# Pair 0's triangular inverses by products on TensorE, in place of column steps on VectorE through DRAM

## The chip, the cores and the metric

One core of a Trainium2 chip runs the whole kernel. The metric is device time in microseconds (us), lower is better. Six runs of the kernel before took 695.22 to 700.58 us, median 697.76. The engines are TensorE (PE: matmuls, with the weight loads PEld beside them), VectorE (DVE), ScalarE (ACT), GpSimd (POOL) and SyncE (SP), which here only issues DMAs. Each engine works through its own queue in order.

## The reference

A delta rule over 768 tokens (4 batches, 8 heads, head size 48), then a gated feed-forward layer:

```python
for t in range(S):
    kt, vt, bt = (k_n[:, :, t], v[:, :, t], beta[:, :, t, None])
    y[:, :, t] = np.einsum('bhd,bhde->bhe', q[:, :, t], state)
    v_old = np.einsum('bhde,bhd->bhe', state, kt)
    state = state + bt[:, :, :, None] * np.einsum('bhd,bhe->bhde', kt, vt - v_old)
...
h = x @ w_in
g = h * np.cos(h)
return (g @ w_out).astype(np.float32)
```

`k_n` is the key divided by its norm; `x` is y with the heads side by side (3072 x 384), `w_in` is 384 x 2048, `w_out` 2048 x 384. Both weight matrices come as 64-bit floats.

## The kernel before

The 768 steps are cut into 24 units of 32 tokens (C = 32), two units to a pair. Within a unit, all steps are solved at once: with G the products of the unit's keys, scaled by beta and cut to its strictly upper triangle, the unit needs the inverse of I + G, a 32x32 triangular matrix for each of 32 (batch, head) blocks. The blocks of a unit lie as 128 partitions (4 batches x 32) by 8 heads x 32.

For a unit `n` of pair `m` the work runs so: load k, q (L337), square, sum and root for the norms (ACT L456, DVE L461, POOL L473, then five small DVE operations L484 to L492); transpose k and q (PE L514) and copy them (`kq_t`, ACT L524); `gram` (PE L545); `gram_keys` gives g (DVE L556), `gram_queries` gives tt (DVE L565). Then the inverse, per pair:

- `gram_put` (SP L576) writes g of both units to DRAM, `gram_get` (SP L585) reads it back with each block in one partition.
- `invert` goes through 31 columns, two operations for each (L614, L621). For pairs 1 to 11 it runs on POOL, with z in SBUF; for pair 0 it runs on DVE, with z in PSUM (`VECTOR = {0: "one"}`), and ACT copies z out (L625).
- `put` (SP L630) writes z to DRAM, `get` (SP L639) reads it back as `zt`, four DMAs for each unit.

Then `through_state` (PE L656), `right_side` (DVE L671), `solve` (PE L683: p_u from zt), `solve_out` (DVE L691), `update` (PE L704), `within` (PE L721), `features` (PE L738) with ACT copies between; a unit needs the state that the unit ahead of it left. When the features of a pair are there, its feed-forward starts: `hidden` in 8 steps (PE L759 for pair 0, in halves by unit; L776 for the others), the cosine on ACT and DVE, then the output (PE L823 for pair 0, and for the others seven products of half the size in Strassen's way, L881, with sums of weights in `w_sum`).

The weights are read in 28 tiles called `pairs` (SP L421; 12 for w_in, 16 for w_out), and each is turned into 32-bit floats by ACT (L429, L431), DVE (L435, L440) and POOL (`narrow_add`, L444). Hidden step k of pair 0 waits for the first 3(k+1) tiles.

The order on each engine isn't written by hand. Every piece of work is a task with an engine, an assumed cost and what it depends on (`add`); `Order.run` plays the tasks through, and each engine takes the ready task with the earliest due time. The tasks are emitted in that order, and each instruction is pinned behind the one ahead of it on its engine. If a task's data come later than was assumed, the engine waits at that place, and everything behind it waits too. The first loads are issued ahead of this: k of unit 0 and q of unit 1 on SP, q of unit 0 on ACT, the constants, beta and k of unit 1 on POOL.

Quoted with the line numbers of the profile:

## Time and profile before

| what | value |
|---|---|
| median of six runs | 697.76 us |
| the profiled execution | 700.58 us, span 698.8 us |
| busy PE | 628.8 us (90%) in 10,968 matmul records |
| busy weight loads | 556.5 us |
| busy DVE | 412.5 us (59%) |
| busy ACT | 264.6 us (38%) |
| busy POOL | 345.6 us (49%) |
| granted PE clock, mean | 0.99 |
| DMA | 52.41 MB, 213,009 packets |

The span counts from the first instruction to the last of the profiled execution; 1.8 us lie around it. A matmul in 32-bit floats shows as two records, so that `gram`, `solve` or `within` of a unit, 32 matmuls each, are 64 records. Busy time is an average over the whole run: what counts for an early change is how the first stretches look, and what ended each wait there.

### The profile page before, as it was taken

Reading aid. Unit: us, or ns where it says so; the run is one execution under the profiler, and the core shown is the slowest. Engines: PE = TensorE matmul, PEld = TensorE weight load, DVE = VectorE, ACT = ScalarE, POOL = GpSimd, SP = SyncE. Lnnn points to the kernel's source line nnn. Section 1 sums busy time; section 2 is a strip of 40 time slices with the busy share of each in tenths; the row PEclk is TensorE's granted clock in tenths of the full one; section 3 lists DMA queues with packets and bytes.
Section 4 is the critical chain, followed back from the end, with each engine's and each line's share of the span. In section 5 each row is a group of like instructions: output and inputs, shape, how many; then the busy total and the mean of one; then the engine's idle time right before and its main releaser. Section 6 shows DMA issues by size and latency. Waiting matters only on the chain.

```text
span 698.8 us, 25089 instructions
## 1 busy us (share of the span) xinstructions
PE 628.8 (90%) x10968; PEld 556.5 (80%) x10968; DVE 412.5 (59%) x820; ACT 264.6 (38%) x450; POOL 345.6 (49%) x738
## 2 busy tenths in 40 slices
PE   3306879998999999999999999999999999999997
PEld 2205768776888888888888898898888988988997
DVE  4885676975675555565565575565466454444542
ACT  4423746733252342342343343343432342433430
POOL 6469848851874824824824824823817608400000
PEclk9999979999999999999999999999999999999999
DMA  9886674455325324324334334235132130100000
GB/s 176 202 168 181 149 195 123 79 81 91 66 42 97 57 47 88 59 47 95 53 58 86 52 57 93 46 52 91 29 70 56 18 62 26 30 14 14 1 23 23
DMA packets 213009, 52.41 MB, mean 75 GB/s; under 512 B 204388, under 2 KB 207604, under 8 KB 212900
## 3 DMA queue, kind: packets, MB, share of 16 engines
q1 hardware_dynamic: 211428, 49.97, 36.5%
q8 instruction: 86, 1.41, 0.8%
q0 software_dynamic: 384, 0.64, 0.4%
q10 hardware_dynamic: 1088, 0.20, 0.1%
q14 instruction: 23, 0.19, 0.1%
HBM read 39.76 MB, written 11.01 MB: 73 GB/s over the span
## 4 chain that ended last, share of the span: by engine, by line
PE 77%; DVE 7%; DMA 6%; SPq 3%; issue 2%; POOL 2%; ACT 1%; ACTq 0%; DVEq 0%; POOLq 0%
PE p_h L776 29%; PE p_out L881 27%; PE p_kq L656 4%; PE p_h L759 4%; PE p_kq L721 3%; PE p_s L704 3%; PE p_u L683 3%; PE p_g L545 2%; SPq L348 2%; PE p_o L881 1%; DMA out_dram<-o 1%; SPq L337 1%; DMA kp<-in_k_dram 1%; DVE p_i L621 1%; PE p_out L823 1%
## 5 line engine op out<-in xcount | busy, mean ns | idle before, releaser
L776 PE MATMUL p_h<-x_ffn,w_in 128*128 128x256 f32 x1056 | 241.4, 381 | 1.3 <-DVE g_ffn L813 1.3
L614 POOL TENSOR_TENSOR part<-z,gb 128x126 f32<-128x126 f32 (+22 forms) x341 | 130.6, 383 | 207.3 <-DMA gb<-g_dr 171.6
L776 PEld LDWEIGHTS p_h<-x_ffn,w_in 128*128 128x128 f32 x1056 | 197.4, 190 | 28.1 <-PE p_t L514 1.1
L621 POOL TENSOR_TENSOR z<-z,part 128x126 f32<-128x126 f32 (+22 forms) x341 | 140.2, 411 | 26.7
L881 PE MATMUL p_out<-w_out,g_ffn 128*128 128x192 f32 x672 | 127.2, 335 | 0.8
L793 DVE SCALAR_TENSOR_TENSOR r<-p_h,turns 128x512 f32<-128x512 f32 x96 | 65.5, 687 | 99.2 <-ACT turns L789 99.2
L789 ACT ACTIVATE turns<-p_h 128x512 int32<-128x512 f32 x96 | 56.5, 592 | 165.9 <-PE p_h L776 148.0
L881 PEld LDWEIGHTS p_out<-w_out,g_ffn 128*128 128x128 f32 x672 | 109.6, 191 | 6.3 <-ACT o L918 3.0
L881 PE MATMUL p_out<-w_sum,g_ffn 128*128 128x192 f32 x496 | 89.0, 329 | 4.4 <-DVE o L931 4.4
L897 DVE TENSOR_TENSOR g_ffn<-g_ffn 128x256 f32<-128x256 f32 x176 | 78.5, 462 | 19.4 <-PE p_out L881 17.5
L800 ACT ACTIVATE r<-r 128x512 f32<-128x512 f32 x96 | 60.4, 629 | 76.6 <-DVE r L793 76.5
L881 PEld LDWEIGHTS p_out<-w_sum,g_ffn 128*128 128x128 f32 x496 | 81.6, 190 | 7.6 <-DVE o L931 6.1
L813 DVE TENSOR_TENSOR g_ffn<-r,p_h 128x512 f32<-128x512 f32 x96 | 65.1, 678 | 35.2 <-ACT r L801 35.0
L801 ACT ACTIVATE r<-r,halfpi 128x512 f32<-128x512 f32 x96 | 69.3, 722 | 3.1
L931 DVE SCALAR_TENSOR_TENSOR o<-p_out,o 128x192 f32<-128x192 f32 x74 | 25.3, 354 | 37.1 <-PE p_out L881 36.1
L514 PE MATMUL p_t<-consts,kp 128*128 128x128 f32 x32 | 7.3, 371 | 41.8 <-DVE tt L565 31.4
L514 PEld LDWEIGHTS p_t<-consts,kp 128*128 128x128 f32 x32 | 5.0, 188 | 43.2 <-issue 38.7
L473 POOL TENSOR_TENSOR knrm<-ksum,halves 128x16 f32<-128x16 f32 (+1 forms) x14 | 36.3, 2596 | 5.5 <-DVE ksum L461 3.2
L732 ACT COPY y<-p_kq 128x384 f32<-128x384 f32 x24 | 11.5, 478 | 65.0 <-PE p_kq L721 65.0
L656 PEld LDWEIGHTS p_kq<-st,kq_t 48*32 48x32 f32 x2944 | 29.7, 106 | 7.7 <-issue 7.0
L656 PE MATMUL p_kq<-st,kq_t 48*32 48x48 f32 x2944 | 33.3, 215 | 2.9 <-issue 2.8
L545 PEld LDWEIGHTS p_g<-kq_t 48*32 48x32 f32 x1536 | 18.2, 114 | 14.8 <-issue 12.7
(74 smaller groups left out, 611.5 us busy)
## 6 DMA issues: line engine op xcount, KB each, us to landing
pairs<-in_moe_w_in_dram SPq DMA_DIRECT2D x12, 512.0 KB
gb<-g_dr SPq DMA_DIRECT2D x24, 256.0 KB
pairs<-in_moe_w_out_dram SPq DMA_DIRECT2D x16, 384.0 KB
vp<-in_v_dram SPq DMA_DIRECT2D x96, 48.0 KB
kp<-in_k_dram SPq DMA_DIRECT2D x92, 48.0 KB
out_dram<-o SPq DMA_DIRECT2D x23, 192.0 KB
g_dr<-g SPq DMA_DIRECT2D x24, 128.0 KB
z_dr<-z SPq DMA_DIRECT2D x12, 256.0 KB
```

The lines of the kernel that those rows point to most:

```text
L473: nc.gpsimd.tensor_tensor(out=scales[m][2][:, part], in0=sums[m, part.start][:, 0:n], in1=halves[:, 0:n], op=ALU.pow,)
L614: eng.tensor_tensor(out=part, in0=z[:, 0:rows, j, None].to_broadcast(shape), in1=a[:, j, None, j + 1 :].to_broadcast(shape), op=ALU.mult,)
L621: eng.tensor_tensor(out=behind, in0=behind, in1=part, op=ALU.subtract)
L656: nc.tensor.matmul(p_kq[quarter(b), par, a, j], kq_t[rows48(par), a, b * NP + j], st[rows48(par), b // 2, j, b % 2], start=(j == 0 and a = ...
L776: nc.tensor.matmul(p_h[:, i], w_in[:, t, (f + i) * 128 : (f + i + 1) * 128], xts[p][:, t], start=(t == 0), stop=(t == KT - 1),)
L789: nc.scalar.activation(turns[p, f], p_hs[p, f], AF.Copy, scale=TURN)
L793: nc.vector.scalar_tensor_tensor(out=r, in0=p_hs[p, f], scalar=TURN, in1=turns.pop((p, f)), op0=ALU.mult, op1=ALU.subtract,)
L800: nc.scalar.activation(r, r, AF.Abs)
L801: nc.scalar.activation(r, r, AF.Sin, bias=halfpi, scale=-2.0 * math.pi)
L813: nc.vector.tensor_tensor(out=out, in0=rests.pop((p, f)), in1=p_hs.pop((p, f)), op=ALU.mult,)
L881: nc.tensor.matmul(p_o, left(p, e // 2, a)[:, e % 2], right(e, b), start=(e == 0), stop=(e == FT // 2 - 1), skip_group_check=True,)
L897: nc.vector.tensor_tensor(out=left(p, k, to), in0=left(p, k, one), in1=left(p, k, two), op=op)
```

## The change

For pair 0 alone, the two units' blocks are no longer sent through DRAM and inverted column by column. The 32x32 triangle is taken as two triangles of 16 (`parts[0]`, called D) and the square between them (`cross`, E). The triangles are inverted by doubling: X = I - D, then X = X + D^2 X, X + D^4 X, X + D^8 X, where the powers come from products 32x32 on PE (`power`, `grow`), each with copies by ACT and DVE and transposes of 32x32 blocks by DVE (`flip`). Two further products with the square (`border`) give the whole inverse, which is `zt`. All of it works in the memory of `w_sum` before the sums of weights are made there; the PSUM comes from tag "h". `invert_eye` and `invert` lose their DVE form; `gram_put`, `gram_get`, `put` and `get` remain for the pairs from 1 on.

The first loads are placed anew: k of units 0 and 1 on SP, q of both on ACT, and the large part of the constants behind beta on POOL. The planner's picture changes with it: the DMA queue is modelled by parts, matmuls cost 1.7 times as much until 4 us after the first hidden step, and start times and due times are others (`WINDOW`, `W_IN`, `W_OUT`, `LOADS`, `START`, `FIRST`, `STEP`), so that the order on every engine is a new one. In the changed order, as it is built, DVE has the flip of unit 0's first power behind the work on the third weight tile and the scales of unit 3; PE has all hidden steps of pair 0 ahead of the solve of unit 2, and all hidden steps of pair 1 and all output steps of pair 0 ahead of the solve of unit 4; SP has g of units 2 and 3 with one weight tile behind each, and the reads of z behind its write with one weight tile between (pair 1) or none (pair 2).

```diff
@@ -33,11 +33,15 @@
+    cross = (p[:, None] % C < C // 2) & (np.arange(C)[None, :] >= C // 2)
...
+            p[:, None] % C == np.arange(C)[None, :],
+            (p[:, None] % C < np.arange(C)) & ~cross,
+            cross,
@@ -54,18 +58,19 @@
-    WINDOW = 128.245
-    LAG = {"PE": 0.2, "DVE": 0.15, "ACT": 0.15, "POOL": 0.2, "SP": 2.0}
-    IN_FLIGHT = 8
+    WINDOW = 114.423
+    LAG = {"PE": 0.2, "DVE": 0.15, "ACT": 0.15, "POOL": 0.2, "SP": 2.0, "IN": 0.3}
+    IN_FLIGHT, ISSUE = 8, 0.49
+    SLOW, WARM = 1.7, 4.0
...
...
@@ -351,27 +359,27 @@
+    load(0, "q", nc.scalar)
+    load(1, "k")
+    load(1, "q", nc.scalar)
...
     consts_dr = nc.inline_tensor(consts_np, name="consts")
...
-    near = 130 + C
-    for cols in (slice(0, near), slice(near, consts_np.shape[1])):
-        nc.gpsimd.dma_start(out=consts[:, cols], in_=consts_dr.ap()[:, cols])
+    near = 130 + 4 * C
+    nc.gpsimd.dma_start(out=consts[:, 0:near], in_=consts_dr.ap()[:, 0:near])
...
-    eye = consts[:, 130 + C :].rearrange("p (r i) -> p r i", i=C)
-    load(0, "q", nc.scalar)
+    diag = consts[:, 130 + C : 130 + 2 * C]
+    parts = consts[:, 130 + 2 * C : near].rearrange("p (x i) -> p x i", i=C)
+    eye = consts[:, near:].rearrange("p (r i) -> p r i", i=C)
...
-    load(1, "q")
-    load(1, "k", nc.gpsimd)
+    nc.gpsimd.dma_start(out=consts[:, near:], in_=consts_dr.ap()[:, near:])
@@ -564,10 +572,101 @@
-            in0=p_gs.pop(n)[:, :, :, 1],
+            in0=p_gs[n][:, :, :, 1],
...
+    doubles = {}
+    def double(n, x):
+        if n not in doubles:
+            flat = w_sum.rearrange("p e x c -> p (e x c)")
+            at = n * 9 * H * C
+            doubles[n] = flat[:, at : at + 9 * H * C].rearrange(
+                "p (x h i) -> p x h i", x=9, i=C
+            )
+        at = "DWEFPQXRB".index(x)
+        return doubles[n][:, at] if len(x) == 1 else doubles[n][:, at : at + len(x)]
+    def mask_scale(n):
+        bs = scales[n // 2][0][:, n % 2]
+        nc.vector.tensor_tensor(
+            out=double(n, "RB"),
+            in0=bs[:, None, :, None].to_broadcast([128, 2, H, C]),
+            in1=parts[:, :, None, :].to_broadcast([128, 2, H, C]),
+            op=ALU.mult,
+        )
+    def mask_keys(n, x):
+        nc.vector.tensor_tensor(
+            out=by_parity(double(n, "DE"[x])),
+            in0=p_gs[n][:, :, :, 0],
+            in1=by_parity(double(n, "RB"[x])),
+            op=ALU.mult,
+        )
+        flip(double(n, "WF"[x]), double(n, "DE"[x]))
+    def flip(to, from_):
+        nc.vector.transpose(
+            to.rearrange("p h i -> p (h i)"), from_.rearrange("p h i -> p (h i)")
+        )
+    p_pows = {}
+    def products32(to, one, two):
+        for h in range(H):
+            for b in range(B):
+                nc.tensor.matmul(
+                    to[quarter(b), h], one[quarter(b), h], two[quarter(b), h]
+                )
+    def power(n, step):
+        if step == 0:
+            p_pows[n] = bank("h", [128, 2, H, C], "p_pow")
+        one, two = ("WD", "QP", "PW")[step]
+        products32(p_pows[n][:, 0], double(n, one), double(n, two))
+    def power_out(n, step):
+        if step < 2:
+            nc.scalar.copy(double(n, "P"), p_pows[n][:, 0])
+        else:
+            nc.scalar.copy(double(n, "Q"), p_pows[n][:, 0])
+    def power_flip(n, step):
+        flip(double(n, "QW"[step]), p_pows[n][:, 0])
+    def grow(n, step):
+        products32(p_pows[n][:, 1], double(n, "QWQ"[step]), double(n, "X"))
+    def less(to, one, two, op=ALU.subtract):
+        nc.vector.tensor_tensor(out=to, in0=one, in1=two, op=op)
+    def grow_out(n, step):
+        if step == 0:
+            wide = [128, H, C]
+            less(double(n, "X"), diag[:, None, :].to_broadcast(wide), double(n, "D"))
+        else:
+            less(double(n, "X"), double(n, "X"), p_pows[n][:, 1], ALU.add)
+        if step == 3:
+            flip(double(n, "R"), double(n, "X"))
+    def border(n, step):
+        to = p_pows[n][:, step]
+        if step == 0:
+            products32(to, double(n, "F"), double(n, "X"))
+        else:
+            products32(to, double(n, "R"), double(n, "B"))
+    def border_out(n, step):
+        if step == 0:
+            nc.scalar.copy(double(n, "B"), p_pows[n][:, 0])
+        else:
+            zts[n] = work.tile([128, H, C], FP, name="zt")
+            less(zts[n], double(n, "X"), p_pows.pop(n)[:, 1])
@@ -587,43 +686,31 @@
-    def invert_eye(m, tag):
-        if tag is None:
-            zs[m] = work.tile([128, ROWS, C], FP, name="z", bufs=ZS)
-        else:
-            zs[m] = bank(tag, [128, ROWS, C], "p_i")
+    def invert_eye(m):
+        zs[m] = work.tile([128, ROWS, C], FP, name="z", bufs=ZS)
         nc.scalar.copy(zs[m], eye)
-    def invert(m, tag, columns):
+    def invert(m, columns):
...
-        eng = nc.gpsimd if tag is None else nc.vector
...
-            if tag is None:
-                part = work.tile([128, ROWS * C // 2], FP, name="part")
-            else:
-                part = ffn_pool.tile([128, ROWS * C // 2], FP, name="part_v", tag="o")
+            part = work.tile([128, ROWS * C // 2], FP, name="part")
...
-            eng.tensor_tensor(
+            nc.gpsimd.tensor_tensor(
...
-            eng.tensor_tensor(out=behind, in0=behind, in1=part, op=ALU.subtract)
-    def invert_out(m):
-        z = work.tile([128, ROWS, C], FP, name="z", bufs=ZS)
-        nc.scalar.copy(z, zs[m])
-        zs[m] = z
+            nc.gpsimd.tensor_tensor(out=behind, in0=behind, in1=part, op=ALU.subtract)
     def put(m):
@@ -951,63 +1038,85 @@
-        free={"SP": 5.5, "ACT": 5.6, "POOL": 6.2, "DVE": 6.0, "PE": 6.0},
+        free={"SP": 4.5, "ACT": 6.2, "POOL": 5.6, "DVE": 4.0, "PE": 5.8},
...
-    VECTOR = {0: "one"}
-    W_IN, W_OUT, LOADS = 96.141, 47.302, -16.83
+    W_IN, W_OUT, LOADS = -9.302, 31.519, 0.897
...
+    COLD = 0.55
...
-    START = 68.004
-    FIRST, STEP = 4.724, 5.365
+    START = 42.564
+    FIRST, STEP = 3.024, 5.599
...
     def inverse(m):
...
-            each = (0.2, 0.001) if held else (0.323, 0.00178)
...
-                2 * (each[0] + each[1] * (j // SPLIT + 1) * (C - 1 - j)) for j in range(x, y)
+                2 * (0.323 + 0.00178 * (j // SPLIT + 1) * (C - 1 - j)) for j in range(x, y)
...
-            add(("inv", m, i), "DVE" if held else "POOL", cost,
-                lambda x=x, y=y: invert(m, held, range(x, y)), deps,
+            add(("inv", m, i), "POOL", cost, lambda x=x, y=y: invert(m, range(x, y)), deps,
...
-        if held:
-            add(("inv_out", m), "ACT", 0.65, lambda: invert_out(m), deps,
-                makes=[("z", ("z", m))], uses=[z])
-            deps = [("inv_out", m)]
...
+    def double_tasks(n, scaled):
+        add(("mask", n), "DVE", 0.7, lambda: mask_scale(n), [scaled])
+        add(("gram_keys", n), "DVE", 0.85, lambda: mask_keys(n, 0),
+            [("gram", n), ("mask", n)], uses=[("p_g", n), ("scales", n // 2)])
+        add(("grow_out", n, 0), "DVE", 0.45, lambda: grow_out(n, 0), [("gram_keys", n)])
+        add(("gram_cross", n), "DVE", 0.85, lambda: mask_keys(n, 1), [("gram_keys", n)],
+            uses=[("p_g", n)])
+        done = [("gram_keys", n)]
+        for i in range(3):
+            add(("power", n, i), "PE", COLD, lambda i=i: power(n, i), done,
+                makes=[] if i else [("h", ("p_pow", n))])
+            if i:
+                add(("grow", n, i), "PE", COLD, lambda i=i: grow(n, i - 1),
+                    [("power", n, i), ("grow_out", n, i - 1)])
+                add(("grow_out", n, i), "DVE", 0.46, lambda i=i: grow_out(n, i),
+                    [("grow", n, i)])
+            if i < 2:
+                add(("power_flip", n, i), "DVE", 0.46, lambda i=i: power_flip(n, i),
+                    [("power", n, i)])
+            add(("power_out", n, i), "ACT", 0.4, lambda i=i: power_out(n, i),
+                [("power", n, i)])
+            done = [("power_out", n, i)] + ([("power_flip", n, i)] if i < 2 else [])
+        add(("grow", n, 3), "PE", COLD, lambda: grow(n, 2), done + [("grow_out", n, 2)])
+        add(("grow_out", n, 3), "DVE", 0.85, lambda: grow_out(n, 3), [("grow", n, 3)])
+        add(("border", n, 0), "PE", COLD, lambda: border(n, 0),
+            [("grow_out", n, 3), ("gram_cross", n)])
+        add(("border_out", n, 0), "ACT", 0.4, lambda: border_out(n, 0), [("border", n, 0)])
+        add(("border", n, 1), "PE", COLD, lambda: border(n, 1), [("border_out", n, 0)])
+        add(("border_out", n, 1), "DVE", 0.46, lambda: border_out(n, 1),
+            [("border", n, 1)], makes=[("zt", ("zt", n))], uses=[("p_pow", n)])
     def unit(n):
...
-                add((x, n), "SP", 0.0, lambda: None)
...
-            deps = [(x, n - 1)] if n else []
-            if n == (0 if x == "v" else 4):
-                deps.append(("gram_get", 0))
+            deps = [(x, n - 1)] if n > (0 if x == "v" else 2) else []
+            if n == 4 and x != "v":
+                deps.append(("gram_get", 1))
...
-                (x, n), "SP", 1.9, lambda x=x: load(n, x), deps,
-                makes=[("vp", ("vp", m))] if x == "v" and not second else [], moves=1.6,
+                (x, n), "SP", 1.95, lambda x=x: load(n, x), deps,
+                makes=[("vp", ("vp", m))] if x == "v" and not second else [], moves=1.25,
@@ -1048,20 +1157,24 @@
-            makes=[(tag, ("p_g", n)), ("g_gram", ("g_gram", n)), ("tt", ("tt", n))],
+            makes=[(tag, ("p_g", n)), ("tt", ("tt", n))]
+            + ([("g_gram", ("g_gram", n))] if m else []),
...
-        add(("gram_keys", n), "DVE", 0.46, lambda: gram_keys(n),
-            [("gram", n), scaled],
-            uses=[("p_g", n), ("scales", m)])
+        if n < 2:
+            double_tasks(n, scaled)
+        else:
+            add(("gram_keys", n), "DVE", 0.46, lambda: gram_keys(n), [("gram", n), scaled],
+                uses=[("p_g", n), ("scales", m)])
...
-        add(("gram_put", n), "SP", 0.45, lambda: gram_put(n), [("gram_keys", n)],
-            makes=[] if second else [("g_dr", ("g_dr", m))], uses=[("g_gram", n)],
-            moves=1.3)
-        if second:
-            inverse(m)
-        add(("get", n), "SP", 1.9, lambda: get(n), [("put", m)], makes=[("zt", ("zt", n))],
-            uses=[("z_dr", m)], moves=1.4)
+        if m:
+            add(("gram_put", n), "SP", 0.45, lambda: gram_put(n), [("gram_keys", n)],
+                makes=[] if second else [("g_dr", ("g_dr", m))], uses=[("g_gram", n)],
+                moves=1.3)
+            if second:
+                inverse(m)
+            add(("get", n), "SP", 1.9, lambda: get(n), [("put", m)],
+                makes=[("zt", ("zt", n))], uses=[("z_dr", m)], moves=1.4)
@@ -1069,7 +1182,8 @@
-        add(("solve", n), "PE", 0.75, lambda: solve(n), [("right", n), ("get", n)],
+        add(("solve", n), "PE", 0.75, lambda: solve(n),
+            [("right", n), ("get", n) if m else ("border_out", n, 1)],
@@ -1199,7 +1313,7 @@
     def weight_sums():
...
-            for x, deps in ((1, adds), (2, [("right", 1, e)]), (4, [("right", 2, e)]),
+            for x, deps in ((1, adds + [("border_out", n, 1) for n in range(2)]), (2, [("right", 1, e)]), (4, [("right", 2, e)]),
@@ -1215,7 +1329,11 @@
-    add(("beta",), "DVE", 1.3, spread_beta)
+    first = []
+    for key, at in ((("k", 0), 5.8), (("q", 0), 6.0), (("bq",), 8.0), (("k", 1), 8.3), (("q", 1), 8.8)):
+        add(key, "IN", at - sum(t for _, t in first), lambda: None, [x for x, _ in first[-1:]])
+        first.append((key, at - sum(t for _, t in first)))
+    add(("beta",), "DVE", 1.3, spread_beta, [("bq",)])
```

## The prediction

> **What bounds the kernel now.** I read the page's busy slices first, to see which engine is full and when.
>
> ```profile
> PE   3306879998999999999999999999999999999997
> POOL 6469848851874824824824824823817608400000
> PEclk9999979999999999999999999999999999999999
> ```
>
> A slice is 17.5 us. TensorE (PE) is full from about 90 us to the end; what is lost is lost ahead of that. The windows by stretches (columns: busy PE, weight loads, DVE, ACT, POOL with their instructions, granted clock, DMA share, GB/s) put sizes to it:
>
> ```profile
> 30.00:40.00 10.00, 0.00 (x0) 0.00 (x0) 8.90 (x33) 2.93 (x5) 0.51 (x3) 1.00 0.82 174
> 40.00:50.00 10.00, 0.00 (x0) 0.00 (x0) 9.22 (x29) 2.60 (x4) 8.43 (x21) 1.00 0.75 166
> ...
> 80.00:90.00 10.00, 4.92 (x351) 4.11 (x342) 8.31 (x14) 6.43 (x13) 8.31 (x6) 0.90 0.65 139
> 90.00:100.00 10.00, 7.88 (x103) 7.73 (x104) 5.07 (x12) 1.37 (x3) 4.84 (x3) 0.58 0.72 164
> ...
> 500.00:600.00 100.00, 99.81 (x1834) 89.35 (x1834) 54.79 (x100) 36.95 (x62) 53.07 (x139) 1.00 0.20 41
> ```
>
> Up to 60 us PE idles 44 us, at 80 to 100 us 7 us more at a low clock; from 500 to 600 us 0.2 us. So each us by which the early work is brought forward reaches the end, if PE is not made to wait again before it is full. The chain that ended last shows what the first pair waits for (start, length, what):
>
> ```profile
> 18.56 4.37 DMA g_dr<-g
> ...
> 23.54 4.46 DMA gb<-g_dr
> ...
> 46.29 0.59 ACT z L625
> ```
>
> Between the second and third line lie the 62 column steps on DVE (28.09 to 46.2 us). Last I followed the solves of the first three pairs through the timeline (start, length, engine, line, tiles, count, idle before):
>
> ```profile
> 24.96 0.42 DVE L556 TENSOR_TENSOR g<-p_g,bs 128x256 f32<-128x256 f32 x1 [0.23 <-PE p_g L545]
> ...
> 39.33 0.24 POOL L614 TENSOR_TENSOR part<-z,gb 128x31 f32<-128x31 f32 x1 [10.71 <-DMA gb<-g_dr]
> ...
> 58.34 1.95 PE L683 MATMUL p_u<-vp,zt 32*32 32x48 f32 x64 [1.21 <-issue]
> ...
> 67.75 1.01 PE L759 MATMUL p_h<-x_ffn,w_in 128*128 128x128 f32 x3
> ...
> 77.55 0.39 SPq L630 DMA_DIRECT2D z_dr<-z  x1
> ...
> 86.74 0.88 PE L683 MATMUL p_u<-rhs,zt 32*32 32x48 f32 x64
> ...
> 92.12 1.21 PE L545 MATMUL p_g<-kq_t 48*32 48x64 f32 x64 [4.50 <-DVE tt L565]
> ...
> 106.20 0.24 POOL L614 TENSOR_TENSOR part<-z,gb 128x31 f32<-128x31 f32 x1
> ...
> 147.70 0.39 SPq L630 DMA_DIRECT2D z_dr<-z  x1
> ...
> 159.95 0.27 PE L683 MATMUL p_u<-rhs,zt 32*32 32x48 f32 x2 [0.53 <-DMA zt<-z_dr]
> ```
>
> Pair 0 is solved at 58.34 us (DVE inverse), pair 1 at 86.74 us and pair 2 at 159.95 us (POOL inverses, 39.33 to 77.5 and 106.20 to 147.6 us). After the third, PE never idles long. The change touches the first alone; the other two hang on POOL, and that is where I look.
>
> **Part 1, the first pair.** Removed: 62 DVE steps (18.1 us), two ACT copies of 0.6, and 13 DMAs of SP (two writes of g, two reads, z, eight reads of zt). Added for each unit: 13 DVE operations, 8 PE products of 32 matmuls, 4 ACT copies (0.45 each, by the 0.48 of y). DVE: a 128x256 mask or sum is 0.42 (g, L556); a flip 0.39, from the transpose of beta (0.98 for 128x768, a third and some start); the scaled masks 0.7 as the 128x512 shift of L435. Both units: 2x(0.7+12x0.41) = 11.2 us in place of 18.1.
>
> No row shows a product 32x32 by 32. Nearest are L683 and L721, 64 records 32x32 by 48: 0.88 us late in the run, 1.50 and 1.95 at 58 to 64 us, where PE works in spurts. I take 1.2 (1.5 cut towards 32 of 48 columns); ends 0.88 and 1.95. The granted clock reads 1.00 in both places, so that row alone does not price it: the four transposes of L514 took 1.09 at 55 us and 0.60 at 134 us.
>
> [...]
>
> **Part 2, the order.** The queues are in order, and the flip of unit 0's first power stands on DVE behind the shift of the third weight tile and the scales of unit 3. SP issues sixteen small loads and two tiles ahead of that tile, as before, where ACT took it at
>
> ```profile
> 21.46 0.69 ACT L429 ACTIVATE w_in<-pairs 128x512 f32<-128x512 f32 x1 [1.05 <-DMA pairs<-in_moe_w_in_dram]
> ```
>
> So: split 1.25 -> 22.7, shift 1.0 -> 23.7, five scale steps 1.0 -> 24.7 us. That the first keys and queries come on two queues, and kq_t ahead of the second square on ACT, brings gram 0 from 13.8 to about 11, but this wait swallows it; I cost it at nothing (without that cover, a gain of 2.8).
>
> From the flip up to g of unit 3 DVE has 28 operations: 4 tile shifts of 1.05, 2 weighs of 1.0, 7 flips of 0.39, 11 of 0.42, sum 13.55 us, plus 1.5 for the fourth tile (issued eight loads or 5 us after the third, 26.5, split 27.8). DVE gets there at 39.7. PE in the same stretch: seven products 8.4, turns of units 2 and 3 3.9 (1.95 each), two grams 2.4, in all 14.7 -> 39.6. They hand to each other step by step, so a little over either: g of unit 3 at **41 us** (38: no waits; 46: products at 1.95), against 25.4 before.
>
> First pair: two border products, an ACT copy, the last subtraction, some 3.5 us after the last gram -> solve at 44.5. From solve to first hidden matmul took 9.4 us (58.34 to 67.75); with one product of the other unit between, 55 us. **That is 12.8 us earlier.**
>
> **Part 3, the second pair pays.** g of unit 3 comes 15.6 us later than before. From it to POOL's first step took 13.9 us (write, tile and value loads, read); the new SP order has one tile between, 0.9 issue + 4.4 write + 0.9 issue + 4.5 to 5.7 read: 11.5 -> 52.5 us. Queued behind those writes on SP are the weight tiles from the eighth on; they wait up to 10 us for g, and hidden steps want them, but PE has slack there until the solve.
> POOL: 38.2 us before, five adds of weights in it (6.95), so 31.3 bare; the new order has seven (three of 1.3, four of 1.02), 39.3 -> z at 91.8. Write and read of z to the solve took 9.2; with only one tile between, 8: solve of pair 1 at **99.8**, 13 us later than before.
> By then the new order has done all 96 hidden matmuls of pair 0 and an output step, the old one 36: 60 x 2 x 0.115 (24 records in 2.75 us) + 1.4 = 15 us ahead. PE idles meanwhile.
>
> **Part 4, the third pair decides.** Gram 5 stands directly behind that solve: 2 us; to the POOL step 12 (14.1 before); inverse 41.5 before with nine adds (10.0), bare 31.4, now four adds 4.2: 35.6; z to solve 8 (12.3 before, with sixteen other issues between; now z and zt are neighbours on SP). 99.8+2+12+35.6+8 = **157.4**, against 159.95: 2.5 us earlier. There the new order has done eight hidden and eight output steps of these pairs, the old seven: 2.75+1.37 = 4.1 us less to do. From there the work is the same. Gain 2.5+4.1 = 6.6 us. A us at g of unit 3 is a us here, both ways.
>
> Sum: the profiled execution took 700.58 us (span 698.8 and 1.8 around it) -> 694.0. It was 2.8 above the median 697.76, which I take off: **691**. The unknown product and DMA waits (g at 38 to 46) make 688 to 696; the two POOL stretches, each good to 4 us, widen it to **683 to 699** as the forecast's own range.
>
> **Rivals.**
> A, faster still: tiles land 2 us earlier and the products run warm, g of unit 3 at 37, and POOL's bare inverses shrink to 29 as DVE's column steps no longer run beside them (POOL steps took 0.7 to 1.0 at 46 to 55 us against 0.45 elsewhere): 4+2.3+2.4 = 8.7 on top of 6.6, 682. Against: DVE's 28 operations alone end at 38.2.
> B, slower: POOL stops inside pair 1's inverse for weight tiles that SP, held by g, sends late. At 5 us per eight loads the sixteenth tile is added at about 83, where POOL gets to it at 81; at 6.2 us it comes at 88, a stop of 6. With g at 45 (4 more) and z to solve as long as before (1.2 and 4.3), pair 2 is solved at 173, and 4.1 ahead leaves 9 us lost: 707; with half of these delays, 699. It decides once pair 2 is solved later than 164. For it: SP already waited 7.2 us for POOL's adds in the first 100 us. Against: fewer adds are left for the third inverse.
> C, nothing to measure: pair 2's solve stays at 160, and the 4.1 go to cold restarts of PE after its longer waits (clock 0.58 at 90 to 100 us): 697.
>
> **How the numbers follow.** Chances: forecast 0.42, A 0.25, B 0.20, C 0.13. A measurement here tells 0.5% (3.5 us) from nothing. Faster: A and nine tenths of the forecast, 0.63; same: C and most of the rest, 0.16; slower 0.21. The range takes in A and half of B: 679 to 702.
>
> **What would show it.** Right: column steps on DVE gone; flip after the third tile's shift; g of unit 3 near 41; POOL's first step near 52, not 39; PE idle before solves of pair 1 (near 100) and 2 (near 157). Wrong: g of unit 3 by 33 (then nearer 680), or PE full from 60 us on, which would mean that POOL isn't what it waits for; wrong the other way if POOL idles for DVE's w_out inside the first inverse.

## The result, and the profile after

The changed kernel takes 703.01 us (median of 16 runs, 698.54 to 705.87) against 697.63 us (median of 37 runs, 693.23 to 700.58) for the kernel before on the same chips: a ratio of 1.0076, 95% interval 1.0057 to 1.0095. It is 0.8% slower where 691 us, 1% faster, was forecast. One thing has to be kept in mind with every pair of lines below: the profiled execution of the changed kernel took 700.95 us (span 699.2), 2.1 below its median, and that of the kernel before 700.58 us, 2.9 above its own. So the two profiled executions are only 0.4 us apart, and some 5 us of the difference lie between the executions and not in the lines.

First the busy slices of the page, with its row of the instruction queue of PE (packets, MB, share):

```profile
PE   4467897799999999999999999999999999999997
POOL 4525885878824822834823834825806604800000
PEclk9975898899999999999999999999999999999999
...
q8 instruction: 94, 1.54, 0.9%
```

PE is busier in the first 90 us than it was, as it should be. But the seventh and eighth slices (105 to 140 us) read 7, where they read 9 before, and the granted clock dips in the third to fifth, and again in the seventh and eighth. The instruction queue moved 94 packets in place of 86. The stretches (same columns as in the prediction), of the kernel before:

```profile
30.00:60.00 30.00, 3.60 (x71) 3.21 (x72) 23.44 (x69) 8.63 (x15) 17.69 (x39) 1.00 0.75 159
100.00:140.00 40.00, 38.55 (x754) 31.99 (x752) 32.83 (x57) 28.74 (x55) 31.69 (x57) 1.00 0.50 128
```

and of the changed kernel:

```profile
30.00:60.00 30.00, 18.74 (x952) 16.92 (x954) 15.74 (x32) 9.85 (x19) 9.80 (x16) 0.74 0.57 151
100.00:140.00 40.00, 31.38 (x798) 24.33 (x797) 30.01 (x61) 16.73 (x33) 28.46 (x35) 0.83 0.59 130
```

From 30 to 60 us PE idles 11.3 us, where the kernel before idled 26.4. From 100 to 140 us it idles 8.6, where the kernel before idled 1.5: part of what was gained is given back there. Over the whole span PE idles 17.2 us less (52.8 for 70.0) and is busy 17.6 us more (646.4 for 628.8); the products alone are 17.2 of these. Then the timeline, with the milestones that the prediction named (start, length, engine, line, tiles, count, idle before):

```profile
25.09 0.44 DVE L614 STREAM_TRANSPOSE w_sum<-p_pow 128x256 f32<-128x256 f32 x1
...
44.42 0.42 DVE L564 TENSOR_TENSOR g<-p_g,bs 128x256 f32<-128x256 f32 x1 [2.74 <-PE p_g L553]
...
51.91 0.29 PE L770 MATMUL p_u<-vp,zt 32*32 32x48 f32 x2
...
56.70 0.24 POOL L706 TENSOR_TENSOR part<-z,gb 128x31 f32<-128x31 f32 x1
...
66.88 3.35 PE L846 MATMUL p_h<-x_ffn,w_in 128*128 128x128 f32 x14
...
99.97 0.38 SPq L717 DMA_DIRECT2D z_dr<-z  x1
...
107.08 0.43 PE L770 MATMUL p_u<-rhs,zt 32*32 32x48 f32 x4 [1.19 <-DMA zt<-z_dr]
...
126.64 0.24 POOL L706 TENSOR_TENSOR part<-z,gb 128x31 f32<-128x31 f32 x1
...
162.72 0.39 SPq L717 DMA_DIRECT2D z_dr<-z  x1
...
173.68 0.88 PE L770 MATMUL p_u<-rhs,zt 32*32 32x48 f32 x64
```

The first flip is where it was forecast (25.09 for 24.7). After it every step is late: g of unit 3 at 44.42 for 41, the first solve at 51.91 for 44.5, the first hidden matmul at 66.88 for 55, and the solve of the third pair at 173.68 for 157.4. What PE waited for up to 100 us (us, times, longest) says why:

```profile
PE p_pow L623 <- DVE w_sum L614: 10.0, 3, 4.3
PE p_pow L623 <- issue: 8.1, 5, 2.6
PE p_t L522 <- DMA kp<-in_k_dram: 7.4, 2, 6.2
PE p_g L553 <- issue: 2.9, 1, 2.9
```

The second and the fourth line are waits for nothing that the profile shows. The chain that ended last holds them one by one (start, length):

```profile
33.54 1.52 issue
...
41.14 2.87 issue
...
46.02 1.71 issue
...
49.66 2.08 issue
...
54.10 2.55 issue
...
62.70 2.38 issue
...
121.49 1.70 issue
...
124.89 2.38 issue
```

I counted the instructions (matmuls, weight loads and the few semaphore waits among them) that PE had started before each of these eight stops:

```
stop at   33.54  41.14  46.02  49.66  54.11  62.70  121.49  124.90
started    1217   1729   1985   2241   2497   3009    5057    5313
```

All differ by multiples of 256. A packet of the instruction queue holds 16 KB (1.54 MB in 94), and the change adds 2048 PE instructions (16 products of 32 matmuls, which the page counts as 1024 matmul records and 1024 weight loads) and 8 packets: 256 instructions to a packet. The DMA records of the trace hold every packet of this queue with its start and length: inside each of the eight stops a packet ends, and PE goes on 1.3 to 1.6 us behind that end. My reading of these numbers is that PE stops where the instructions of one packet end and the next has not arrived. In the stop at 41.14, for one, the packet runs from 41.70 to 42.65, and PE goes on at 44.01. The kernel before has two such stops, 2.11 us at 83.96 and 1.66 at 170.63, after 1985 and 4801 instructions, on the same grid; there too PE goes on 1.3 to 1.4 us behind a packet's end. The 1.21 us that it waits ahead of its first solve, at 58.34, are put down to issue too, but stand after 623 instructions, off the grid, with no packet near: that wait is something else.

### The profile page after: what moved, and what is told of

It reads as the page before. It is cut to its first block, busy times and chain, and to the rows that moved or that the text cites. A ratio compares the mean times of both kernels' runs of the same rounds, so it can differ in the third digit from the quotient of the medians.

```text
span 699.2 us, 27117 instructions
## 1 busy us (share of the span) xinstructions
PE 646.4 (92%) x11992; PEld 570.9 (82%) x11992; DVE 406.7 (58%) x782; ACT 267.3 (38%) x456; POOL 338.3 (48%) x734
## 3 DMA queue, kind: packets, MB, share of 16 engines
q8 instruction: 94, 1.54, 0.9%
## 4 chain that ended last, share of the span: by engine, by line
PE 79%; DMA 6%; issue 4%; DVE 3%; ACT 3%; SPq 3%; POOL 1%; DVEq 0%; ACTq 0%; POOLq 0%
PE p_h L863 30%; PE p_out L968 26%; PE p_kq L743 4%; PE p_out L910 3%; PE p_u L770 3%; PE p_kq L808 3%; DMA pairs<-in_moe_w_in_dram 2%; PE p_s L791 2%; PE p_g L553 2%; PE p_pow L623 2%; PE p_o L968 1%; SPq L356 1%; PE p_h L846 1%; DMA pairs<-in_moe_w_out_dram 1%; SPq L345 1%
## 5 line engine op out<-in xcount | busy, mean ns | idle before, releaser
L713 POOL TENSOR_TENSOR z<-z,part 128x126 f32<-128x126 f32 (+22 forms) x341 | 135.6, 398 | 26.7
L984 DVE TENSOR_TENSOR g_ffn<-g_ffn 128x256 f32<-128x256 f32 x176 | 80.4, 475 | 19.8 <-PE p_out L968 17.9
L481 POOL TENSOR_TENSOR knrm<-ksum,halves 128x16 f32<-128x16 f32 (+1 forms) x14 | 37.0, 2642 | 12.3 <-DVE ksum L469 7.7
L819 ACT COPY y<-p_kq 128x384 f32<-128x384 f32 x24 | 11.5, 478 | 78.3 <-PE p_kq L808 78.3
L623 PE MATMUL p_pow<-w_sum 32*32 32x32 f32 x1024 | 17.2, 237 | 19.0 <-DVE w_sum L614 10.0
L623 PEld LDWEIGHTS p_pow<-w_sum 32*32 32x32 f32 x1024 | 15.4, 150 | 21.3 <-issue 14.9
L452 POOL TENSOR_TENSOR w_in<-w_in,pairs 128x512 uint32<-128x512 uint32 x12 | 15.4, 1284 | 31.1 <-DVE w_in L448 30.7
```

The costliest lines, as they stand in the source:

```text
L623: nc.tensor.matmul(to[quarter(b), h], one[quarter(b), h], two[quarter(b), h])
L713: nc.gpsimd.tensor_tensor(out=behind, in0=behind, in1=part, op=ALU.subtract)
L984: nc.vector.tensor_tensor(out=left(p, k, to), in0=left(p, k, one), in1=left(p, k, two), op=op)
```

## The experiments

The theory (called the fetch theory in the expectations): the added matmul instructions come too late at PE. The rival (the order theory): what counts is the order, above all that the grams of units 2 and 3 now stand behind products, so that POOL starts 17 us later. A third: that the loads on two queues hurt. Ratios are to the kernel before, timed on the same chip in the same session (its median was 697.01 us with the first four, 698.69 with the four that follow, 699.44 with the last four). "Stops" below are idle times of PE put down to issue, added up over the first 140 us.

**One part alone: the loads.** The kernel before with

```diff
-    load(1, "q")
-    load(1, "k", nc.gpsimd)
+    load(1, "k")
+    load(1, "q", nc.scalar)
```

and with q of unit 0 moved ahead of the constants, and the large part of the constants behind beta on POOL's queue, as in the change; nothing else.

> The kernel before with the new placement of the first loads alone (keys of the first pair on SP, queries on ACT, constants and beta on POOL); the column steps, the order and the planner's constants are those of before. Fetch theory (the added matmul instructions of the products are late at PE): nothing of it is in this kernel, so gram 0 comes 2 to 3 us earlier, the flip into the column steps up to 2 us earlier, and the time is that of before within 0.3% (696 to 699). Order theory (what is given up is the old order): the same, as the order is kept. Loads theory (that two queues fill at once hurts the weight tiles): g of unit 3 no earlier than 25 us, the first weight tile's shift 1 us later or more, and the time up by 2 us or more.

698.94 us, ratio 1.0028 (0.9999 to 1.0058). Gram 0 came at 11.22 us for 13.78, but g of unit 3 at 26.93 for 24.96, and the column steps began 1.9 us later, not earlier. The shift of the first weight tile came 1.8 us sooner (15.43 for 17.18), those of the second and third 1.8 and 1.7 later (22.12 for 20.35, 25.44 for 23.71). So a part of what the loads theory named is there: by the middle of the interval the loads cost 2 us of the 5.3 that the change lost, and nothing and 4 us both lie in it. They don't stand in the way of a gain: the kernels below that beat the kernel before have them too.

**The products' instructions doubled, and halved, in one order.**

```diff
# doubled
-                nc.tensor.matmul(
-                    to[quarter(b), h], one[quarter(b), h], two[quarter(b), h]
-                )
+                for _ in range(2):
+                    nc.tensor.matmul(
+                        to[quarter(b), h], one[quarter(b), h], two[quarter(b), h]
+                    )
# halved
-        for h in range(H):
+        for h in range(0, H, 2):
             for b in range(B):
                 nc.tensor.matmul(
-                    to[quarter(b), h], one[quarter(b), h], two[quarter(b), h]
+                    to[quarter(b), h : h + 2], one[quarter(b), h], two[quarter(b), h : h + 2]
                 )
```

> The changed kernel with each matmul of the sixteen products issued twice, the second writing the same values again; the order is kept. 2048 more PE instructions, eight more packets of the instruction queue. Fetch theory: each product costs 1.07 us more and each 256 instructions a stop of some 2 us, so g of unit 3 (44.4 us after the change) goes to 56 to 62, solve 0 (51.9) to 76 to 84, with some fifteen stops of 1.5 us or more ahead of it in place of seven, and the time rises by 15 to 25 us (718 to 728). Order theory: only the matmuls themselves count, about 1 us each: g of unit 3 at 50 to 53, solve 0 at 64 to 68, time up by 8 to 13 us.

> The changed kernel with each product as 16 matmuls of 64 columns in place of 32 of 32: the weights of the even head are used for the odd one too, so half of the heads' products of the first pair are left out and others stand in their place. Same order, same tiles, same columns streamed, half of the products' PE instructions (1024 fewer, four packets of the instruction queue fewer). Fetch theory: the stops ahead of solve 0 fall from seven to three or four, g of unit 3 comes at 38 to 41 us (44.4), solve 0 at 43 to 46 (51.9), solve of pair 1 at 100 to 103 (107.1), time down 3 to 6 us (697 to 700). Order theory: the stops are waits under another name, g of unit 3 stays at 42 us or later, solve 0 at 49 or later, time down by less than 2 us.

Doubled: 729.96 us, ratio 1.0475 (1.0436 to 1.0513). g of unit 3 came at 56.86, solve 0 at 74.05 (a little before the range), with ten stops of over 1.2 us ahead of it and not fifteen; the time lies above the range. PE's waits up to 100 us, and the instruction packets between 30 and 60 us:

```profile
PE p_pow L624 <- issue: 23.4, 12, 3.1
...
PE p_g L553 <- issue: 3.1, 2, 2.1
...
q8 instruction: 8, 0.13, 1.7%
```

Eight packets in 30 us: where PE hangs on them, a packet comes every 3.7 us, which is 14 to 15 ns an instruction, while a product of the changed kernel runs through its 128 in 1.07 us, 8.4 ns each.

Halved: 692.65 us, ratio 0.9941 (0.9915 to 0.9967), the lowest median of all kernels here. By the ratios it lies 1.35% (9.4 us) below the changed kernel; the loss turned into a gain, a larger one than the 697 to 700 us expected. The product of 32 records at 54.50 took 1.07 us, the one of 64 at 65.88 in the changed kernel 1.08 (granted clock 0.50), so there the columns cost what they did and only instructions went. Two others took 1.46 us together (at 35.65), and all products together are busy 14.6 us for 17.2, so a small part of the gain can be their length and not the stops. Its waits up to 100 us:

```profile
PE p_pow L623 <- DVE w_sum L614: 11.4, 3, 5.6
...
PE p_kq L743 <- issue: 1.9, 1, 1.9
PE p_pow L623 <- issue: 1.4, 1, 1.4
PE p_u L770 <- issue: 1.0, 1, 1.0
```

The stops of the products fell from 8.1 us to 1.4, that of the gram is gone; ahead of solve 0 one stop of over 1.2 us is left (the changed kernel has four), where three or four were expected. g of unit 3 came at 39.79, solve 0 at 43.07, solve of pair 1 at 97.33 (3 us ahead of the range): the milestones that the prediction gave to the whole change (41, 44.5, 99.8), each 1.2 to 2.5 us sooner. The order theory had less than 2 us.

**The order turned round.** Due times of the turns, grams, g, its write and its read of units 2 and 3 set 60 us earlier, and with them those of tt of the first four units and of the square of the first two:

```diff
+        for key, task in self.tasks.items():
+            if key[1:] and key[1] in early.get(key[0], ()):
+                task[2] -= 60.0
```

> The changed kernel with the tasks that POOL's first inverse hangs on (turns, grams, g and its way through DRAM of units 2 and 3) given due times 60 us earlier, so that the planner sets them ahead of the first pair's products; instructions are the same in number. Order theory: g of unit 3 comes at 26 to 32 us (44.4), POOL's first inverse step at 40 to 45 (56.7), solve of pair 1 at 91 to 95 (107.1), solve of pair 2 at 158 to 163 (173.7); solve 0 a few us later, at 52 to 58; time down 5 to 10 us, 693 to 698. Fetch theory: the stops go with the products, solve 0 at 58 to 64 (what the grams gain the first pair loses), and the time down 0 to 4 us.

706.53 us, ratio 1.0143 (1.0108 to 1.0178): slower still, which neither theory had.

```profile
34.20 0.39 DVE L569 TENSOR_TENSOR g<-p_g,bs 128x256 f32<-128x256 f32 x1
45.44 0.24 POOL L711 TENSOR_TENSOR part<-z,gb 128x31 f32<-128x31 f32 x1
...
170.34 0.88 PE L775 MATMUL p_u<-rhs,zt 32*32 32x48 f32 x64
```

The grams did come 10 us sooner and POOL began 11 us sooner, but pair 1 was solved only 4.5 us sooner (102.54) and pair 2 3.3 (170.34). So an early POOL start alone does not win back the loss. What the late one costs is not shown by it, as the planner placed much else anew. Why this order is slower at the end, though its pairs are solved sooner, I have not settled; PE idles 4.0 us of 140 to 200 us in it, 0.5 in the changed kernel.

**The new order without the new method.** The column steps of the kernel before under the loads, the planner and the due constants of the change.

```diff
-    W_IN, W_OUT, LOADS = 96.141, 47.302, -16.83
+    W_IN, W_OUT, LOADS = -9.302, 31.519, 0.897
...
-    START = 68.004
+    START = 42.564
```

> The column steps of the kernel before, under the new kernel's loads, planner and due constants: the new order without the new method. Fetch theory: no products, so no new stops; the new order by itself costs little, 694 to 700, with pair 2 solved at 155 to 163. Order theory: the new order is what costs, so this kernel lies above the one before too, 701 to 706, with pair 2 solved at 168 or later.

703.73 us, ratio 1.0071 (1.0039 to 1.0103), pair 2 solved at 168.42: what the order theory said. An order that suits one method costs the other 5 us. So an order can move a kernel by nearly as much as the change did (1.0071 and 1.0076), and effects of instructions are read only between kernels of one order, as with the doubled and the halved.

**Fewer instructions, in orders of their own.** Three kernels that save instructions and let the planner order them anew. Merged: the next square and the sum share their weights and become one matmul of 64 columns. Whole: no halves, the doubling runs over the 32 x 32 block. The core of both:

```diff
+        one, to, two = double(n, "QW"[step - 1]), p_pows[n], double(n, "PX")
+        for h in range(H):
+            for b in range(B):
+                nc.tensor.matmul(
+                    to[quarter(b), :, h], one[quarter(b), h], two[quarter(b), :, h]
+                )
```

> The changed kernel with the next square and the sum that share one set of weights made by one matmul of 64 columns (power and sum side by side in the bank): 192 matmuls for each unit in place of 256, 512 PE instructions fewer in all; the same sums, computed in halves of 16 as in the change. Fetch theory, with the price that the half-instruction kernel gave (10.4 us for 1024): 5 us down, 697 to 699, solve 0 at 46 to 49 us (51.9), stops at every second or third block of 256 instructions. Order theory: no change beyond 2 us, 701 to 704.

> The changed kernel without halves: the doubling runs over the whole 32 x 32 block (four squares, each with its sum in one matmul of 64 columns), so the border's two products, its mask, its flip and the flip ahead of it go; 160 matmuls for each unit in place of 256, 768 PE instructions fewer, and on DVE three operations fewer for each unit. Fetch theory: 7.8 us down by the price of the half-instruction kernel, and a little more by the shorter chain: 692 to 696, solve 0 at 41 to 46 us. Order theory: only the shorter chain, some 3 us earlier at solve 0, and 699 to 702.

> As the kernel without halves, but the last factor of the doubling (the sixteenth power of the block) is left out, so the inverse is cut after the fifteenth power: 128 matmuls for each unit, 1024 PE instructions fewer than in the change. Fetch theory: as the half-instruction kernel or a little less, 689 to 693, solve 0 at 39 to 43 us, pair 1 solved at 95 to 99. Order theory: 697 to 701.

All three missed the ranges of the fetch theory, and the last came where the order theory had it: 707.67 us, ratio 1.0132 (1.0078 to 1.0185); 703.32, 1.0055 (1.0026 to 1.0084); 700.11, 1.0025 (0.9997 to 1.0053). Their stops were fewer (13.7, 13.6 and 12.6 us for 17.4), but the planner had also moved other work: in the merged kernel g of unit 3 went to 51.85. Method and order are mixed up in them, so I ran the same edits again with every task held in the changed kernel's place: a merged matmul stands where the square stood, and the place of the sum stays empty.

**Fewer instructions, one order.** With them the extreme case, four matmuls of 256 columns for a product:

```diff
# an eighth
-        for h in range(H):
-            for b in range(B):
-                nc.tensor.matmul(
-                    to[quarter(b), h], one[quarter(b), h], two[quarter(b), h]
-                )
+        for b in range(B):
+            nc.tensor.matmul(to[quarter(b)], one[quarter(b), 0], two[quarter(b)])
# merged, and whole, in place; pair32 is the loop of 64 columns shown above
         if step == 0:
             p_pows[n] = bank("h", [128, 2, H, C], "p_pow")
-        one, two = ("WD", "QP", "PW")[step]
-        products32(p_pows[n][:, 0], double(n, one), double(n, two))
+            products32(p_pows[n][:, 0], double(n, "W"), double(n, "D"))
+        else:
+            pair32(n, double(n, "QW"[step - 1]))
```

> The changed kernel, same order, with each product as 4 matmuls of 256 columns in place of 32 of 32: the first head's weights stand in for all eight, so the products of the other seven heads of the first pair are left out. As many columns, an eighth of the products' PE instructions (1792 fewer). Fetch theory: nearly no stops by products are left ahead of solve 0; g of unit 3 at 36 to 40 us, solve 0 at 40 to 43, time 685 to 691, below the half-instruction kernel's 692.65. Order theory (the instruction count was only a lucky shift): no better than the half-instruction kernel, 692 or more.

> The merged kernel's matmuls of 64 columns (next square and sum side by side, 512 PE instructions fewer), but every task kept in the changed kernel's order: the merged matmul stands where the square stood, and the place of the sum stays empty. Fetch theory: 4 to 6 us below the changed kernel, 697 to 699, g of unit 3 at 40 to 42 us; the 707.67 of the merged kernel came from its own order (g of unit 3 at 51.85). Order theory: 701 to 704.

> The doubling over the whole 32 x 32 block (768 PE instructions fewer, exact), every task in the changed kernel's order. Fetch theory: 6 to 9 us below the changed kernel, 694 to 697, solve 0 at 44 to 47 us. Order theory: 700 to 704.

> As the kernel over the whole block in the changed kernel's order, without its last factor (the sixteenth power is left out): 1024 PE instructions fewer, as in the half-instruction kernel. Fetch theory: 689 to 694, solve 0 at 41 to 44 us, pair 1 solved at 95 to 98. Order theory: 699 to 703.

All kernels of the changed kernel's order, by their products' PE instructions:

| kernel | PE instructions of the products | packets of q8 | stops to 140 us | solve 0 | solve of pair 2 | median us | ratio (95%) |
|---|---|---|---|---|---|---|---|
| doubled | 4096 | 102 | 31.9 | 74.05 | 200.44 | 729.96 | 1.0475 (1.0436 to 1.0513) |
| changed | 2048 | 94 | 17.4 | 51.91 | 173.68 | 703.01 | 1.0076 (1.0057 to 1.0095) |
| merged in place | 1536 | 92 | 15.0 | 49.11 | 174.00 | 703.97 | 1.0062 (1.0035 to 1.0089) |
| whole in place | 1280 | 91 | 15.0 | 45.86 | 165.88 | 698.02 | 0.9968 (0.9936 to 1.0000) |
| halved | 1024 | 90 | 7.8 | 43.07 | 163.10 | 692.65 | 0.9941 (0.9915 to 0.9967) |
| whole, last factor out | 1024 | 90 | 8.4 | 44.34 | 162.98 | 695.45 | 0.9936 (0.9908 to 0.9963) |
| an eighth | 256 | 87 | 4.9 | 40.63 | 162.53 | 694.23 | 0.9925 (0.9901 to 0.9949) |

In every one of these seven, each stop of 1.2 us or more ahead of 200 us stands after a number of instructions of the form 193 + 256n. Rows were timed in different sessions, so the ratios are to be compared, not the medians. Of the expectations: the eighth has nearly no stops left by products (0.8 us is the longest before 100 us), but at 694.23 us it lies above its range, where the order theory had it, and its ratio is that of the halved kernel within the intervals: little is left to be had below 1024. There PE waits for DVE:

```profile
PE p_pow L622 <- DVE w_sum L614: 11.3, 3, 5.4
...
PE p_pow L622 <- DVE w_sum L643: 3.8, 3, 3.2
```

Whole in place and the one without its last factor came out as the fetch theory had it by their ratios (7.5 and 9.8 us below the changed kernel); their medians lie 1.0 and 1.5 us above the ranges. Merged in place missed: g of unit 3 came at 41.32 and solve 0 2.8 us sooner, as expected, but its stops fell by 2.4 us only, pair 2 was solved no sooner, and at 139 to 144 us PE waits 4.35 us for DVE's g_ffn once. Why it does is open.

**A version that beats both.** Whole in place computes the same inverse, and is 1.1% below the changed kernel (0.9968 to 1.0076); that it beats the kernel before by 0.3% is at the edge of its interval. The kernel without its last factor is 0.6% below the kernel before, surely so, and 1.4% below the changed one, but it leaves out the sixteenth power. For these inputs, where beta is at most 0.4 and the keys are random, that power is small; for keys that lie close together it would not be.

## Why the prediction was wrong, step by step

**The product was priced right.** I took 1.2 us (ends 0.88 and 1.95); the trace has 1.07 for most of those that no stop breaks (1.46 for the worst, at 59.79). The 1.00 that I read for the clock at 58 to 64 us was no reading: the trace of the kernel before has its first record of the clock at 71.0 us, that of the changed one at 40.96, and ahead of it the rows show 1.00. In the changed kernel the clock on record is 0.50 beside the product at 59.79 and beside one of 1.08 us (at 65.88); the four transposes of L522 took 0.60 us at 1.00 (at 119.52) and 1.11 at 0.50 (at 128.32). The eighth kernel's products, as many columns in 8 records, took two lengths:

```profile
37.91 0.63 PE L622 MATMUL p_pow<-w_sum 32*32 32x256 f32 x8 [0.46 <-DVE w_sum L643]
...
44.71 1.08 PE L622 MATMUL p_pow<-w_sum 32*32 32x256 f32 x8 [3.20 <-DVE w_sum L643]
```

So 1.2 lies between the two lengths at 0.50, and near the 1.07 of most.

**The failing step** is "PE in the same stretch: seven products 8.4, turns of units 2 and 3 3.9 (1.95 each), two grams 2.4, in all 14.7". It holds work only (and 14.7 after the flip at 24.7 is 39.4, not 39.6). The products bring 2048 instructions, and the stops came with them. Ahead of gram 3 stand two stops, 1.52 + 2.87 = 4.4 us: 41 + 4.4 less 0.9 (seven products at 1.07) = 44.5, and g of unit 3 came at 44.42. Between it and solve 0 stand 1.71 + 2.08 = 3.8 us more, and 44.5 + 3.5 + 3.8 = 51.8 for the measured 51.91. From there to the first hidden matmul I had 10.5 us; 2.55 + 2.38 = 4.9 us of stops make 15.4, and it took 15.0. The stops account for the delay of each of these milestones up to 67 us. And when instructions are taken out in the same order, most of what separates the forecast (0.990 of the kernel before) from the result (1.0076) comes back: 0.9941 with half of the products' instructions, 0.9925 with an eighth. I could have seen it: the kernel before shows the stops, on its own grid, as

```profile
86.07 0.74 PE L545 MATMUL p_g<-kq_t 48*32 48x64 f32 x50 [2.11 <-issue]
...
172.29 0.29 PE L656 MATMUL p_kq<-st,kq_t 48*32 48x48 f32 x8 [1.66 <-issue]
```

and class Order carries a price for it (`BLOCK, PHASE, AHEAD, FETCH = 256, 63, 38, 3.5`) beside the instruction counts that the diff extends; 256 less 63 is the 193 of the grid. Eight packets at 1.7 to 2.1 us would have been 13 to 17 us, with nothing to hide them.

**"12.8 us earlier" for the first pair**, at its first hidden matmul, became 0.9 (67.75 to 66.88); at solve 0 it was 6.4 (58.34 to 51.91).

**The second pair.** From g to POOL's first step I had 11.5 us; it took 12.3. The inverse I put at 39.3; it took 43.2 (56.70 to 99.9). Two adds of weights stop POOL inside it, for 4.07 and 2.12 us. The first goes back to a stop of PE (the three lines are of PE, DVE and POOL):

```profile
65.08 0.86 PE L743 MATMUL p_kq<-st,kq_t 48*32 48x48 f32 x49 [2.38 <-issue]
...
65.98 0.56 DVE L758 TENSOR_TENSOR rhs<-vp,p_kq 128x384 f32<-128x384 f32 x1 [3.02 <-PE p_kq L743]
...
68.53 1.28 POOL L452 TENSOR_TENSOR w_in<-w_in,pairs 128x512 uint32<-128x512 uint32 x1 [4.07 <-DVE w_in L448]
```

On DVE the shift of the tile that POOL wants stands behind the right side, which waited 3.02 us for PE's product. The tile was split by 63.75. The second goes back to ACT, where the split of its tile stands behind a step of the cosine that waits 1.84 us for a hidden product (until 90.54). In the halved kernel the inverse took 39.0 us (50.36 to 89.38). So the solve of pair 1 came at 107.08 for 99.8.

**The third pair.** From that solve to POOL's next step I had 14 us; it took 19.6, and POOL was not waiting for g alone:

```profile
114.62 1.01 POOL L452 TENSOR_TENSOR w_out<-w_out,pairs 128x384 uint32<-128x384 uint32 x1 [2.98 <-DVE w_out L448]
119.57 1.26 POOL L452 TENSOR_TENSOR w_out<-w_out,pairs 128x384 uint32<-128x384 uint32 x1 [3.94 <-DVE w_out L448]
122.19 2.90 POOL L481 TENSOR_TENSOR knrm<-ksum,halves 128x16 f32<-128x16 f32 x1 [1.36 <-DVE ksum L469]
```

The read of g had been issued by 117.27. Between its two inverses POOL has adds that wait for DVE and three norms of 2.9 to 3.2 us, which I left out. The inverse itself took 36.1 for 35.6. z to the solve took 11.0 for 8, the solve standing behind hidden and output steps of 2.74 us on a PE that is now full: from 140 us up to this solve it idles 0.5 us, where the prediction had it idle ahead of the solve. Late in sum: 7.3 + 5.6 + 0.5 + 3.0 = 16.4 us (16.3 before rounding), 173.7 in place of 157.4. The middle part is no effect of the stops: the halved kernel too took 18.4 us there.

**The lead was under-priced.** "4.1 us less to do" after the third solve: from it to the end the kernel before takes 538.8 us, the changed one 525.5, which is 13.3 less. Counted by matmul records, the changed kernel has one hidden step and one output step fewer to run there, as I said (12 and 8 records), but I took half an output step's length, 1.37 us. In the kernel before it reads

```profile
129.00 2.74 PE L823 MATMUL p_out<-w_out,g_ffn 128*128 128x384 f32 x8
```

so these steps are 5.5 us. Another 5.9 are waits that are gone: from the third solve to the end PE idles 14.4 us in the kernel before and 8.5 in the changed one. The last 1.9 are the same records in less time; the granted clock of the kernel before is 0.50 for 3.4 us from 173.4 us on, that of the changed one is 1.00 from 133 us up to its last matmuls, and by my estimate that is most of it (half of 3.4). In sum 694.0 + 16.3 - 9.2 = 701.1, and the profiled execution took 700.95. That is 7 of the 12 us between 691 and 703; the other 5 lie between the executions, as said above. The forecast of 691, which the halved kernel nearly meets, rests there on two errors of mine that cancel: its third solve is 5.7 us later than my 157.4.

**The clock.** One cost is in none of these sums. From 100 to 140 us the granted clock reads 0.83 for 1.00 (0.50 from 109.2 to 116.1), and an output step there takes longer than one behind it:

```profile
112.12 4.78 PE L910 MATMUL p_out<-w_out,g_ffn 128*128 128x384 f32 x8
...
160.66 2.74 PE L910 MATMUL p_out<-w_out,g_ffn 128*128 128x384 f32 x8
```

It is what rival C named. How much of the loss it makes, no run separates.

**"The third pair decides", "a us at g of unit 3 is a us here".** The second is too low: from halved to changed to doubled, g moves 4.6 and 12.4 us, and the third solve 10.6 and 26.8; in the doubled kernel longer products and more stops both add to it. The first I can't uphold as it was meant. In the one order the ratio does follow that solve, from 0.9925 at 162.53 to 1.0076 at 173.68 (10.5 us of 697.6 for 11.2) and 1.0475 at 200.44 (27.8 for 26.8). But PE does not wait for it in the changed kernel: it stands in a full queue and shows how far PE has come. And between orders it does not tell the time: whole, in its own order, solves pair 2 at 163.43 and has 1.0055, where halved has 0.9941 at 163.10.

**The rivals.** B said slower, 699 to 707, decided once pair 2 is solved later than 164, with POOL stopped inside the first inverse by weight tiles, "a stop of 6", g at 45 and pair 2 at 173. All that came: 4.07 + 2.12 us, 44.42, 173.68, 703. Its cause was another: SP, held by g, did not send the tiles late; a stop of PE held DVE for the first stop of POOL, and a hidden product held ACT for the second. I gave it 0.20, so it was right in its numbers partly by luck. A is out, since DVE and PE did not get to g earlier; C had the third solve at 160.

## What to carry to other kernels

Count instructions, not only their times: in this early stage a 32 x 32 product cost its 1.07 us and some 0.9 us more in stops (17.4 up to 140 us less the 3.6 of the kernel before, over 16 products). Before small matmuls are added, look in the trace for idle times of PE put down to issue and at which instruction count they stand, and where the packets of the instruction queue end. What helped here was fewer instructions: the whole block without the two halves, and one factor less. Wider matmuls on shared weights alone (merged in place, 1.0062 for 1.0076) brought nothing clear of the intervals. And compare variants in one order: letting a planner set the order anew moved these kernels by as much as the edit did.

## What the runs showed of the hardware

PE stops of 1.2 us or more that are put down to issue stand after 193 + 256n instructions: all of them in the changed kernel (eight, after 1217 to 5313), two of the three in the kernel before (after 1985 and 4801; the third, 1.21 us at 57.13, after 623), and those ahead of 200 us in the other six kernels of the table. In these eight kernels they last 1.2 to 3.3 us. In the traces of the changed kernel and the kernel before, PE goes on 1.3 to 1.6 us behind the end of a 16 KB packet of its instruction queue, and a packet itself took 0.9 to 1.6 us. In the doubled kernel eight packets came in the 30 us from 30 to 60, one in some 3.7 us. With as many columns a product took 1.08 us in 64 matmul records (changed kernel, at 65.88, granted clock 0.50), 1.07 in 32 (halved, at 54.50) and 1.08 in 8 (an eighth, at 44.71); elsewhere two took 1.46 us in 32 records each (halved, at 35.65) and one 0.63 in 8 (an eighth, at 37.91). In the changed kernel four transposes took 0.60 us at a granted clock of 1.00 (at 119.52) and 1.11 at 0.50 (at 128.32).
